# Unread matmuls and 128-partition operands at the start of an RWKV attention and wave-mixing kernel

## The chip, the cores and the metric

The kernel runs on one core of one Trainium2 chip. The metric is device time in microseconds of one execution. A core has TensorE (PE, matmuls; its weight loads are listed as PEld), VectorE (DVE), ScalarE (ACT), GpSimd (POOL) and SyncE (SP, which here only issues DMAs). Each engine works through its own instruction list in order and waits on semaphores for the others. TensorE writes to PSUM, which this kernel splits into eight banks.

## The reference

Inputs: r, k, v of shape (4, 8, 768, 48) (batch, heads, sequence, head size), w and u of shape (8, 48), a 384x384 matrix w_theta, two 768x768 matrices w_tok_r and w_tok_i, a 384x384 matrix w_ch; all float32.

```python
for t in range(S):                                     # per batch and head
    cur = einsum('bhd,bhe->bhde', u * k[t], v[t])
    y[t] = einsum('bhd,bhde->bhe', r[t], state + cur)
    state = w[:, :, None] * state + einsum('bhd,bhe->bhde', k[t], v[t])
x = y as (4, 768, 384)
theta = x @ w_theta
zr, zi = x * cos(theta), x * sin(theta)
u = x + w_tok_r @ zr + w_tok_i @ zi                    # over the sequence
out = u + max(u @ w_ch, 0)
```

w lies between 0.85 and 0.95. The recurrence is computed in chunks: powers of w are exp(position x log w), r and k are scaled by them, and matmuls take the place of the loop.

## The kernel before

The sequence is cut into 6 chunks of 128 positions; two chunks are one pair, so 4 batches give 12 pairs (g = 0 to 11). For each pair the front part loads k, r and v (tile `ld`), multiplies k and r by tables of powers (`Kw`, `Rw`, line 669), transposes them through TensorE (line 558, function flip) into banks, copies these out to `KT` and `RT` (lines 567 and 569), forms the scores (line 708), multiplies them by a causal mask (`mAT`, line 715), sums the state (lines 754 and 768) and adds past and present (lines 828, 839, 847). For the first four pairs v comes in two positions per row and is put in place by matmuls against a 0/1 matrix `place` (line 633; copied out at 641 and 643). Then theta (line 862), cosine and sine (867, 870), z (873), the mixing over the sequence (893), the residual (900), the channel product (916) and the result (920).

At the start log w must be had on every partition. w is loaded as one row (line 358), its logarithm taken on one partition (`lw_f`, line 409), and the function spread (line 418) multiplies a row of ones (1x128) with that row, in two halves of 192 columns, so that every partition of the bank `lw` holds all 384 values. The tables (line 474) are exponentials of that bank. The function stand (line 451) later puts log w upright for the decay over 256 positions. `w_f` and `lw_f` are rows in memory that later belongs to the tile z of batch 1.

The order of work is not that of the code. Every task is put on a plan with its engine, an estimated length, what it reads and writes, and which PSUM banks it takes. The method order simulates the engines with these estimates and takes, whenever an engine is free, the ready task with the lowest number in a written-out list, RANK. It charges matmuls 1.9 times their length while the plan's time is under SLOW_UNTIL = 10400 ns. The tasks are then issued in that order, each engine's instructions in a fixed sequence. A flag `port` marks VectorE and GpSimd tasks that share a memory port; a dependence is added between them so that they do not meet.

Before the change nothing stands in TensorE's list but work whose result is read.

Of the kernel before, what the change touches and what calls it, by code (L numbers as in the profile page):

```python
# [16 lines left out]
F32 = mybir.dt.float32  # L17
F16 = mybir.dt.float16
BF16 = mybir.dt.bfloat16
# [3 lines left out]
PE, DVE, ACT, POOL, SP = "PE", "DVE", "ACT", "POOL", "SP"  # L23
LAT = {PE: 230.0, DVE: 150.0, ACT: 250.0, POOL: 170.0, SP: 0.0}
SWITCH = 95.0
LANDING = 2000.0
SLOW_UNTIL = 10400.0
TURN_LATE = 1300.0

# [7 lines left out]
class Plan:  # L37
# [50 lines left out]
    def order(self):  # L88
# [15 lines left out]
        def release(xs, at):  # L104
            for x in xs:
                x.ready = max(x.ready, at)
                x.nwait -= 1
                if x.nwait == 0:
                    waiting[x.eng].append(x)
                    heapq.heappush(times, x.ready if x.ready > now else now + 1e-3)  # L110

        while times or dma_next < math.inf:
# [7 lines left out]
            while dma_at < now:  # L120
# [10 lines left out]
                if dma_at + need <= now + 1e-6:  # L131
                    dma_at += need
                    t = queues[q].pop(0)
                    todo[q] = queues[q][0].xfer if queues[q] else 0.0
                    t.end = dma_at + LANDING + (t.share[1] if q == 0 else 0.0)
                    release(t.users, t.end)
                else:
                    dma_at = now
            for e in engines:
# [14 lines left out]
                if e == PE:  # L154
                    ns += SWITCH if t.mode != last_mode else 0.0
                    ns *= 1.9 if now < SLOW_UNTIL else 1.0
                    last_mode = t.mode
# [97 lines left out]
def kernel(  # L255
# [13 lines left out]
    nc = tc.nc  # L269
    B, H, S, D = r.shape  # L270
    HD = H * D
    C = 128
# [7 lines left out]
    sb = ctx.enter_context(tc.tile_pool(name="sb", bufs=1))  # L280
    ps = ctx.enter_context(tc.tile_pool(name="ps", bufs=1, space=bass.MemoryType.PSUM))
    P = Plan(8)
    bank_t = [ps.tile([C, 512], F32, name=f"bank{i}") for i in range(8)]

    def bank(tok):
        return bank_t[P.bank_of[tok]]
# [4 lines left out]
    def ring(n, shape, dt, nm):  # L291
        return [sb.tile(shape, dt, name=f"{nm}{i}") for i in range(n)]
# [4 lines left out]
    pi2 = sb.tile([C, 1], F32, name="pi2")  # L297
# [1 line left out]
    wu = sb.tile([2 * HP, 2, Dp], F32, name="wu")  # L299
    tok_i = sb.tile([C, 1], mybir.dt.int32, name="tok_i")  # L300
    tok_f = sb.tile([C, 6], F32, name="tok_f")
    ones = sb.tile([1, C], F32, name="ones")
    gate = sb.tile([1, 1], F32, name="gate")
    place = sb.tile([C, 2, 2, C], BF16, name="place")
    rpow = sb.tile([C, 2, H, D], F32, name="rpow")
# [26 lines left out]
    zs = ring(2, [C, NCH, 2, HD], BF16, "z")  # L332
# [6 lines left out]
    WrT = sb.tile([C, NCH, S], BF16, name="WrT")  # L339
    WiT = sb.tile([C, NCH, S], BF16, name="WiT")  # L340

    w_f, lw_f = [zs[1].rearrange("p o t n -> p (o t n)")[:1, 2 * i * HD:2 * (i + 1) * HD]
                 .bitcast(F32) for i in range(2)]
    fins = [fin_all[:, i] for i in range(3)]
# [12 lines left out]
    def setup():  # L357
        P.add(SP, 420, lambda: nc.sync.dma_start(out=w_f, in_=w.rearrange("(o h) d -> o (h d)", o=1)),
              wr=["w_f"], prio=-1e7, xfer=-900)
# [6 lines left out]
        def fills():  # L366
            nc.vector.memset(pi2, math.pi / 2.0)
            nc.vector.memset(ones, 1.0)
        P.add(DVE, 120, fills, wr=["pi2", "ones"], prio=-101)
        P.add(ACT, 1400, lambda: nc.scalar.activation(warm, pi2, Act.Ln), wr=["warm"], prio=-99)  # L370

        def tok():
# [18 lines left out]
        def pads(ts):  # L391
            for t in ts:
# [3 lines left out]
              wr=["ident"], prio=-98)  # L396
        P.add(DVE, 200 * len(Rws), lambda: pads(Rws), wr=[("Rw", i) for i in range(len(Rws))],
              prio=-97)
        P.add(DVE, 200 * len(Kws), lambda: pads(Kws), wr=[("Kw", i) for i in range(len(Kws))],
              prio=-96)  # L400

        def mask():
# [1 line left out]
            nc.gpsimd.affine_select(  # L404
                out=mask01, in_=mask01, compare_op=Alu.is_ge, fill=0.0,
                base=-1, channel_multiplier=-1, pattern=[[1, C]])
        P.add(POOL, 600, mask, wr=["mask"], prio=-95)

        P.add(ACT, 550, lambda: nc.scalar.activation(lw_f, w_f, Act.Ln), rd=["w_f"],
              wr=["lw_f"], prio=-98)  # L410

        P.add(ACT, 1400, lambda: nc.scalar.activation(warm, pi2, Act.Exp), rd=["pi2", "lw_f"],
              wr=["warm"], prio=-97)

        for s in range(2):
            def spread(s=s):
                half = slice(s * HD // 2, (s + 1) * HD // 2)
                nc.tensor.matmul(bank("lw")[:, half], ones, lw_f[:, half],
                                 start=(s == 0), stop=(s == 1), skip_group_check=True)
            P.add(PE, 800, spread, rd=["lw_f", "ones"], acq=["lw"] if s == 0 else [],  # L420
                  use=[] if s == 0 else ["lw"], wr=[("lw", s)], prio=-98 + s, name="spread")
# [25 lines left out]
    def late_tables(rd):  # L447
        def stand():
            for h in range(H):
                q = h % 2 * Dp  # L450
                nc.tensor.matmul(bank("lwT")[q:q + D, h // 2:h // 2 + 1],
                                 lw_f[:, h * D:(h + 1) * D], ones[:, :1], start=(h < 2),
                                 stop=(h >= H - 2), skip_group_check=True)
        P.add(PE, 500, stand, rd=["lw_f", "ones"] + rd, acq=["lwT"], prio=3, mode=3,
              name="stand")

        def far():
            for hi in range(2):
                q = slice(hi * Dp, hi * Dp + D)
                nc.scalar.activation(w256[q], bank("lwT")[q, :HP], Act.Exp, scale=float(2 * C))  # L460
        P.add(ACT, 360, far, use=["lwT"], wr=["w256"], prio=3)

        def uw_fill():
            for hi in range(2):
                q = slice(hi * Dp, (hi + 1) * Dp)
                nc.vector.tensor_mul(uw[q, :, hi], wup[q, HP:], wup[q, :HP])
        P.add(DVE, 330, uw_fill, rd=["wup"] + rd, wr=["uw"], prio=3, port=True)
        table("kpow", kpow, 2, 5, rd)

    def table(key, dst, col, prio, rd=(), hs=range(H), s=None):  # L470
        h0, h1 = hs.start, hs.stop
        halves = [s] if s is not None else [0, 1]
        for c in range(2):
            P.add(ACT, act_ns((h1 - h0) * D, False) + 100, lambda c=c: nc.scalar.activation(
                dst[:, c, h0:h1].rearrange("p h d -> p (h d)"), bank("lw")[:, h0 * D:h1 * D],
                Act.Exp, scale=tok_f[:, col + c:col + c + 1]),
                rd=["tok_f"] + [("lw", i) for i in halves] + list(rd), use=["lw"],
                wr=[(key, c, i) for i in halves], prio=prio + 0.1 * c)
# [399 lines left out]
    def mixing(b, base):  # L878
        x, z = xs[b % 3], zs[b % 2]
        xi, zj = b % 3, b % 2  # L880
        for pr in range(NP):
# [42 lines left out]
            for ts_ in parts:  # L924
# [5 lines left out]
                    wr=[("out", b, pr, ts_.start)], prio=-2e6, xfer=520 * n)  # L930

    setup()
    front(0, 0)
    for b in range(B):
# [7 lines left out]
    for t, at in zip(P.tasks, RANK):  # L942
        t.prio = at
    order = P.order()
    made, before = nc.cur_bb.bb.instructions, None
    for t in order:
        n = len(made)
        t.fn()
        if not t.port:
            continue  # L950
        if t.eng == DVE:
            before = made[-1]
        elif before is not None:
            tc.add_manual_dep(made[n], before.name, mybir.DependencyInfo(
                mybir.DependencyClass.Sync, mybir.DependencyReason.DATA), reason="port")
            before = None
# [30 lines left out]
```

## Time and profile before

| What | us |
|---|---|
| three runs | 137.7, 138.62, 138.0 (median 138.0) |
| profiled execution | 138.1 |
| its span, first to last instruction | 136.4 |
| TensorE busy | 125.7 (92%) |
| VectorE busy | 111.1 (81%) |
| ScalarE busy | 73.1 (54%) |
| GpSimd busy | 62.0 (45%) |
| chain that ended last: TensorE, VectorE, DMA | 58%, 12%, 10% |
| read and written in memory off the core | 20.06 MB, 4.72 MB |

Times in the profile count from the first instruction of the span. A matmul's length includes its way through the array, so successive ones overlap; how fast TensorE works is read from the distance between starts, or by comparing matmuls of one shape. "[1.04 <-PE bank L708]" behind a line means that the engine was idle for 1.04 us before it and that the wait ended with TensorE's line 708. The spread's four passes (two halves, float32) start at 2.77 and end at 4.42. The next matmuls are four transposes at 5.83, one of 8 columns at 6.37, and four transposes at 7.47.

### The profile page before, as it was taken

How to read it: one execution, taken by the hardware profiler on the slowest of the kernel's cores; microseconds unless marked ns; L12 is line 12 of the kernel's file. 1: busy time of each engine (PE TensorE's matmuls, PEld its weight loads, DVE VectorE, ACT ScalarE, POOL GpSimd, SP SyncE). 2: the span in 40 equal slices, each digit the busy share in tenths (PEclk: the TensorE clock that was granted, in tenths of full speed). 3: DMA queues.
4: the chain of work that ended last, by engine and by line, in shares of the span. 5: the costliest groups of instructions: out<-in, count | busy, mean ns of one | idle time of the engine just before them, and what ended most of it. 6: DMA issues, size and time to landing. Idle time of an engine off the chain costs nothing.

```text
span 136.4 us, 4100 instructions
## 1 busy us (share of the span) xinstructions
PE 125.7 (92%) x1677; PEld 85.8 (63%) x1677; DVE 111.1 (81%) x209; ACT 73.1 (54%) x137; POOL 62.0 (45%) x54
## 2 busy tenths in 40 slices
PE   1589998999999999999999999999999999999970
PEld 1267876697577677757566666765666666666640
DVE  5199699998988799998999999999955799453390
ACT  7996599999756580687533308556450192500010
POOL 6027979984180658959379937690000000000000
PEclk9999999999999999999999999999999999999996
DMA  2999999999999999999999999989992842526245
GB/s 56 244 325 324 311 191 194 196 200 198 208 189 227 186 176 201 195 187 192 171 126 218 165 214 231 219 215 227 177 289 44 100 117 95 137 82 173 58 153 193
DMA packets 72637, 25.24 MB, mean 185 GB/s; under 512 B 67241, under 2 KB 72618, under 8 KB 72618
## 3 DMA queue, kind: packets, MB, share of 16 engines
q1 hardware_dynamic: 70186, 22.03, 82.5%
q0 software_dynamic: 2432, 2.95, 12.6%
q8 instruction: 13, 0.21, 0.7%
q14 instruction: 6, 0.05, 0.1%
HBM read 20.06 MB, written 4.72 MB: 182 GB/s over the span
## 4 chain that ended last, share of the span: by engine, by line
PE 58%; DVE 12%; DMA 10%; POOL 6%; SPq 6%; issue 5%; ACT 1%; POOLq 0%; ACTq 0%; DVEq 0%
PE bank L893 25%; PE bank L558 11%; PE bank L862 6%; PE bank L916 6%; DMA ld<-in_v_dram 4%; DVE mAT L715 4%; SPq L502 4%; DMA uu_all<-uu_all 3%; POOL Kw L669 3%; DMA ld<-in_r_dram 3%; PE bank L708 2%; PE bank L633 2%; PE bank L839 2%; POOL yd L739 2%; PE bank L768 2%
## 5 line engine op out<-in xcount | busy, mean ns | idle before, releaser
L893 PE MATMUL bank<-z,WrT 128*128 128x384 bf16 x144 | 46.9, 327 | 0.0
L893 PE MATMUL bank<-z,WiT 128*128 128x384 bf16 x144 | 46.8, 326 | 0.0
L715 DVE TENSOR_TENSOR mAT<-bank,mask 128x512 bf16<-128x512 f32 x48 | 30.7, 680 | 2.2 <-PE bank L708 2.1
L669 POOL TENSOR_TENSOR Kw<-ld,kpow 128x768 bf16<-128x768 f32 x9 | 16.3, 1812 | 13.7 <-DVE KT L567 6.1
L900 DVE TENSOR_TENSOR uu_all<-bank,x 128x384 bf16<-128x384 f32 x24 | 13.2, 552 | 8.8 <-PE bank L893 8.3
L893 PEld LDWEIGHTS <-WrT 128*128 128x128 bf16 x144 | 14.0, 97 | 8.0
L893 PEld LDWEIGHTS <-WiT 128*128 128x128 bf16 x144 | 14.1, 98 | 7.8
L669 POOL TENSOR_TENSOR Rw<-ld,rpow 128x768 bf16<-128x768 f32 x9 | 16.3, 1816 | 5.7 <-PE bank L708 2.4
L739 POOL TENSOR_TENSOR yd<-dg,vb 128x768 bf16<-128x768 f32 x10 | 14.7, 1472 | 6.5 <-DVE z L873 3.3
L870 ACT ACTIVATE trig<-bank 128x384 f16<-128x384 f32 x24 | 11.7, 498 | 10.2 <-PE bank L862 10.2
L920 DVE SCALAR_TENSOR_TENSOR fin_all<-bank,uu_all 128x384 f32<-128x384 f32 x24 | 12.6, 550 | 3.4 <-PE bank L916 3.4
L916 PE MATMUL bank<-Wch,uu_all 128*128 128x384 bf16 x72 | 14.7, 327 | 0.1
L867 ACT ACTIVATE trig<-bank,pi 128x384 f16<-128x384 f32 x24 | 13.7, 587 | 1.7 <-PE bank L862 1.7
L862 PE MATMUL bank<-Wth,xT 128*128 128x384 bf16 x72 | 14.4, 327 | 0.0
L873 DVE TENSOR_TENSOR z<-x,trig 128x1536 bf16<-128x1536 bf16 x12 | 13.0, 1084 | 0.4 <-ACT trig L867 0.4
L847 DVE TENSOR_TENSOR x<-bank,yd 128x384 bf16<-128x384 f32 x24 | 12.3, 547 | 0.7 <-POOL yd L739 0.5
L569 ACT ACTIVATE KT<-bank 128x1024 bf16<-128x1024 bf16 (+1 forms) x10 | 9.8, 982 | 5.1 <-PE bank L558 2.5
L569 ACT ACTIVATE RT<-bank 128x1024 bf16<-128x1024 bf16 (+1 forms) x9 | 8.7, 971 | 5.2 <-PE bank L558 5.2
L558 PE MATMUL bank<-ident,Kw 128*128 128x128 bf16 x96 | 8.9, 243 | 1.6 <-DVE Kw L669 1.4
L708 PE MATMUL bank<-RT,KT 64*128 64x128 bf16 x192 | 9.3, 226 | 0.0
L916 PEld LDWEIGHTS <-uu_all 128*128 128x128 bf16 x72 | 6.6, 98 | 4.2 <-DMA uu_all<-uu_all 0.5
L558 PE MATMUL bank<-ident,Rw 128*128 128x128 bf16 x96 | 8.4, 235 | 0.8 <-DVE Rw L669 0.8
(103 smaller groups left out, 186.9 us busy)
## 6 DMA issues: line engine op xcount, KB each, us to landing
ld<-in_r_dram SPq DMA_DIRECT2D x12, 384.0 KB, 5.4
out_dram<-fin_all SPq DMA_DIRECT2D x11, 384.0 KB, 2.7
ld<-in_k_dram SPq DMA_DIRECT2D x16, 192.0 KB, 5.1
ld<-in_v_dram SPq DMA_DIRECT2D x16, 192.0 KB, 4.9
ld<-in_k_dram SPq DMA_DIRECT2D x4, 384.0 KB, 4.8
ld<-in_v_dram SPq DMA_DIRECT2D x4, 384.0 KB, 5.6
fin_all<-in_moe_w_tok_r_dram POOLq DMA_DIRECT2D x1, 384.0 KB, 7.8
x<-in_moe_w_tok_i_dram POOLq DMA_DIRECT2D x1, 384.0 KB, 9.3
```

The lines of the kernel that those rows point to most:

```text
L558: nc.tensor.matmul(bank16(tok)[:, i * C:(i + 1) * C], s, ident, is_transpose=True, start=(i == 0), stop=(i == n - 1))
L569: nc.scalar.activation(dst, src, Act.Copy)
L669: eng.tensor_mul(X[:, :, hs, :D], src[:, :, hs], pw[:, :, hs])
L715: P.add(DVE, dve_ns(HP * C), lambda hi=hi, tk=tk, mAT=mAT: nc.vector.tensor_mul(mAT[:, hi], bank(tk[hi]).rearrange("p (h t) -> p h t", h=H ...
L739: eng.tensor_mul(yd.rearrange("p a h d -> p (a h) d"), wide(dg, D), vb.rearrange("p a h d -> p (a h) d"))
L862: nc.tensor.matmul(bank(th)[:, :HD], xT[:, t, dk, :], Wth[:, dk, :], start=(dk == 0), stop=(dk == ND - 1))
L867: P.add(ACT, act_ns(HD, False) + 65 + (1300 if g == 0 and t == 0 else 0), lambda th=th, t=t, trig=trig: nc.scalar.activation(trig[:, t, 0] ...
L873: P.add(DVE, dve_ns(4 * HD, 2.0) + 80, lambda trig=trig, pr=pr: nc.vector.tensor_mul(z[:, 2 * pr:2 * pr + 2], bc(x[:, 2 * pr:2 * pr + 2], ...
L893: nc.tensor.matmul(bank(tm)[:, :HD], (WrT, WiT)[ri][:, so, to * C:(to + 1) * C], z[:, so, ri], start=(part == 0 and i == 0), stop=(part == ...
L900: P.add(DVE, dve_ns(HD), lambda tm=tm, t=t, to=to, un=un: nc.vector.tensor_add(un[:, t], bank(tm)[:, :HD], x[:, to]), use=[tm], rd=[("x", ...
L916: nc.tensor.matmul(bank(tf)[:, :HD], uT[:, t, dk, :], Wch[:, dk, :], start=(dk == 0), stop=(dk == ND - 1))
L920: nc.vector.scalar_tensor_tensor(fin[:, t], bank(tf)[:, :HD], 0.0, un[:, t], op0=Alu.max, op1=Alu.add),
```

## The change

`ones` becomes 128x128. `lw_all` names all 128 partitions of the memory whose first partition is `lw_f`; VectorE sets it to zero before the logarithm is written there, and the spread multiplies the 128x128 ones with it: 127 of the 128 rows are zero, and the sums are the same. A tile `stuff` (128x256, bfloat16) is filled by GpSimd with 1.0 and, in every second column, -0.5. The function fill issues n matmuls of 256 columns with `stuff` as both operands into a bank that the plan holds to be free at that time; nothing reads the result. Six stand behind the second spread, ahead of the next TensorE task. replay goes once more through the order found by the plan, now charging 1.9 times only while the time is under FREE_FROM = 7400 ns, and notes for each TensorE task from when to when TensorE would wait for it. Ahead of each later task that begins before FILL_UNTIL = 17500 ns in that replay, fill is issued with as many matmuls as fit into the wait at 214 ns each (110 ns from 7400 ns on); these are 15 in all. The order of the tasks is the same as before.

```diff
+FILL_FIRST = 6
+FILL_UNTIL = 17500.0
+FREE_FROM = 7400.0
...
-    ones = sb.tile([1, C], F32, name="ones")
+    ones = sb.tile([C, C], F32, name="ones")
+    stuff = sb.tile([C, 2 * C], BF16, name="stuff")
...
+    lw_all = zs[1].rearrange("p o t n -> p (o t n)")[:, 2 * HD:4 * HD].bitcast(F32)
...
             nc.vector.memset(ones, 1.0)
-        P.add(DVE, 120, fills, wr=["pi2", "ones"], prio=-101)
+            nc.vector.memset(lw_all, 0.0)
+        P.add(DVE, 520, fills, wr=["pi2", "ones", "lw_f"], prio=-101)
...
-        P.add(POOL, 600, mask, wr=["mask"], prio=-95)
+            nc.gpsimd.memset(stuff, 1.0)
+            nc.gpsimd.memset(stuff.rearrange("p (a b) -> p a b", b=2)[:, :, 1], -0.5)
+        P.add(POOL, 1000, mask, wr=["mask"], prio=-95)
...
-                nc.tensor.matmul(bank("lw")[:, half], ones, lw_f[:, half],
+                nc.tensor.matmul(bank("lw")[:, half], ones, lw_all[:, half],
...
-                                 lw_f[:, h * D:(h + 1) * D], ones[:, :1], start=(h < 2),
+                                 lw_f[:, h * D:(h + 1) * D], ones[:1, :1], start=(h < 2),
...
+    held = {}
+    for t in order:
+        for b in t.uses:
+            a, e = held.get(b, (t.start, 0.0))
+            held[b] = (a, max(e, t.end))
+
+    def fill(since, until, n):
+        free = {}
+        for i in range(P.nbanks):
+            spans = [held[b] for b in held if P.bank_of[b] == i]
+            if all(e <= since or a >= until for a, e in spans):
+                free[i] = max([e for a, e in spans if e <= since], default=0.0)
+        if n < 1 or not free:
+            return
+        spare = bank_t[min(free, key=free.get)]
+        for _ in range(n):
+            nc.tensor.matmul(spare[:, :2 * C], stuff[:, :C], stuff, start=True, stop=True)
+
+    def replay():
+        free, done, left, gap, last_mode = dict.fromkeys((PE, DVE, ACT, POOL, SP), 0.0), {}, {}, {}, 0
+        port = 0.0
+        for t in order:
+            at = max([free[t.eng]] + [done[d] for d in t.deps])
+            for b in t.acq:
+                at = max(at, left.get(P.bank_of[b], 0.0))
+            if t.port:
+                at = max(at, port)
+            ns = t.ns
+            if t.eng == PE:
+                gap[t] = (free[PE], at)
+                ns += SWITCH if t.mode != last_mode else 0.0
+                ns *= 1.9 if at < FREE_FROM else 1.0
+                last_mode = t.mode
+            free[t.eng] = at + ns
...
+            done[t] = max(t.end, at) if t.xfer > 0 else at + ns + LAT[t.eng] - min(t.xfer, 0.0)
...
+        return gap
+
+    gap = replay()
+    idle_from, spreads = 0.0, 0
     made, before = nc.cur_bb.bb.instructions, None
     for t in order:
+        if t.eng == PE:
+            if spreads == 2:
+                fill(4e3, t.start, FILL_FIRST)
+            elif spreads > 2 and gap[t][1] < FILL_UNTIL:
+                since, until = gap[t]
+                fill(idle_from, t.start, int((until - since) / (214.0 if until < FREE_FROM else 110.0)))
+            spreads += t.name == "spread" or spreads >= 2
+            idle_from = t.start
         n = len(made)
         t.fn()
```

More of the change, by code (lines that the diff above doesn't have):

```diff
@@ L944 @@
     order = P.order()
+    held = {}
[30 more added lines that the diff above has]
+            free[t.eng] = at + ns
+            if t.port:
+                port = at + ns
+            done[t] = max(t.end, at) if t.xfer > 0 else at + ns + LAT[t.eng] - min(t.xfer, 0.0)
+            for b in t.uses:
+                left[P.bank_of[b]] = max(left.get(P.bank_of[b], 0.0), done[t])
+        return gap
+    gap = replay()
+    idle_from, spreads = 0.0, 0
     made, before = nc.cur_bb.bb.instructions, None
     for t in order:
+        if t.eng == PE:
[6 more added lines that the diff above has]
+            idle_from = t.start
         n = len(made)
```

## The prediction

> **What bounds the kernel now.** I read the page's busy shares and clock row first, then stretches of the span, then TensorE's and VectorE's instructions in order of time, then the chain and the waits. The page:
>
> ```profile
> PE 125.7 (92%) x1677; PEld 85.8 (63%) x1677; DVE 111.1 (81%) x209; ACT 73.1 (54%) x137; POOL 62.0 (45%) x54
> PEclk9999999999999999999999999999999999999996
> ```
>
> TensorE (PE) is busy nearly always, and the clock row shows a full clock from the start. The durations contradict that row. TensorE in order of time (start, length, line, shape; "xN" merges N matmuls):
>
> ```profile
> 10.67 1.46 PE L633 MATMUL bank<-v,place 128*128 128x384 bf16 x4
> ...
> 12.78 0.40 PE L731 MATMUL bank<-uw,PD 128*128 128x2 bf16 x8
> 13.10 0.81 PE L451 MATMUL bank<-ones,z 1*48 1x1 f32 x16
> 13.84 1.18 PE L768 MATMUL bank<-v,Kw 64*64 64x48 bf16 x32
> 14.95 1.03 PE L558 MATMUL bank<-ident,Rw 128*128 128x128 bf16 x8
> 15.91 0.61 PE L708 MATMUL bank<-RT,KT 64*128 64x128 bf16 x8
> ...
> 17.45 1.17 PE L633 MATMUL bank<-v,place 128*128 128x384 bf16 x4
> ...
> 18.86 0.48 PE L633 MATMUL bank<-v,place 128*128 128x384 bf16 x2
> ...
> 20.16 0.62 PE L558 MATMUL bank<-ident,Rw 128*128 128x128 bf16 x8
> ```
>
> Compare like with like. Eight transposes of 128 columns (L558) take 1.03 us at 14.95 and 0.62 us at 20.16. Single L633 matmuls of 384 columns last 525 ns at 17.45 and 17.77, then 368 at 18.09, then 327 at 18.29, and start 320 ns apart before and 160 ns apart after. So TensorE runs at half rate until about 18.2 us and at full rate from there. From 8.48 to 18.09 it has no gap over 0.15 us beyond its own work; the chain of work that ended last lies on matmuls from 7.47 to 19.36 almost without a break. That is 9.6 us at half rate, and up to 4.8 us if all of it ran at full rate. That is the prize. Who would be late next? VectorE (DVE):
>
> ```profile
> 13.65 1.13 DVE L669 TENSOR_TENSOR Kw<-ld,kpow 128x768 bf16<-128x768 f32 x1
> ...
> 15.15 0.36 DVE L805 TENSOR_TENSOR T<-bank,N 128x192 f32<-128x192 f32 x1
> 16.56 1.29 DVE L715 TENSOR_TENSOR mAT<-bank,mask 128x512 bf16<-128x512 f32 x2 [1.04 <-PE bank L708]
> ...
> 19.98 0.56 DVE L643 CAST vb<-bank 128x384 bf16<-128x384 f32 x1 [0.20 <-ACT dg L736]
> ```
>
> Between 8.6 and 20 us VectorE stands idle for TensorE only once worth naming, 1.04 us before the mAT products, and 0.20 us at 19.98. Stretches after that (busy us of PE, PEld, DVE, ACT, POOL):
>
> ```profile
> 20.00:24.00 4.00, 3.61 (x74) 2.65 (x67) 4.00 (x8) 3.72 (x8) 3.91 (x4) 1.00 1.18 192
> 24.00:28.00 4.00, 3.85 (x103) 2.88 (x101) 4.00 (x10) 3.96 (x7) 3.98 (x5) 1.00 1.15 197
> 28.00:49.00 21.00, 21.00 (x300) 15.21 (x297) 18.44 (x31) 15.77 (x28) 11.13 (x8) 1.00 1.13 196
> 49.00:96.00 47.00, 46.17 (x737) 31.66 (x736) 46.24 (x82) 24.35 (x46) 31.94 (x21) 1.00 1.23 198
> ```
>
> From 20 to 28 VectorE is full (8.00 of 8.00) and TensorE is the one that waits. From 28 to 49 TensorE is full, from 49 to 96 both nearly, and after 96 it is a run of matmuls. So time won on TensorE before 18 us passes through VectorE's full stretch: the end moves by what VectorE wins, not by what TensorE wins.
>
> **The change part by part.** All sums are against the profiled execution, 138.1 us (span 136.4, 1.7 around it); the median shown, 138.0, is 0.1 lower.
>
> *Setup fills.* VectorE's new fill of log w is 384 columns on 128 partitions. A 128-column fill (L393) lasts 0.17 and the next begins 0.14 later, so 0.42. Filling `ones` on 128 partitions instead of 1 is free by the rows (1x128, 8x128 and 128x128 all 0.17). VectorE's setup work ends at 2.95 and it is next needed at 5.21, so 0.42 is hidden with 1.8 us to spare. One point is open: SyncE's small w load at 1.71 must follow the fill of wu, which ends at 1.24 and would end at 1.66, just as SyncE's k issue ends (1.67): cost 0. But the chain view ties that load to a VectorE instruction that ends at 2.05; if that is right, every later load slips 0.42. I take 0 (the fill named in the code decides) and keep 0.42. GpSimd's two fills of `stuff`: 0.21 for 128 columns (L403), 0.53 for 512 (L424), so 0.32 plus 0.21 to 0.53 for the strided one. `place` then is ready at 3.8 instead of 3.2 and is first read at 10.67: hidden.
>
> *Spread with 128 rows.* The four passes of L418 (1 row, 192 columns) start 320 ns apart. Rows do not change a start-to-start time elsewhere (L558 with 128 rows: 106 ns per 128 columns at half rate; L708 with 64 rows in pairs: the same). I take no cost; double, 1.65, as the far end would push the first transposes from 5.83 to 6.1.
>
> *Six unread matmuls.* 256 columns are two thirds of an L633 matmul: 213 ns at half rate, 107 at full. Six from about 4.2 are 1.28, done by 5.5; the next matmul starts at 5.83 when VectorE's Kw lands. Cost 0.
>
> *Fifteen more.* 15 x 107 = 1.6 us at full rate, 3.2 us at half. They sit ahead of tasks that the kernel's own plan thinks will wait. At full rate TensorE has about 4.8 us less to do there, so they displace nothing but waiting: 0, at worst the 1.6 us.
>
> *Will the rate rise earlier?* The rows ask what came before 18.2. From 14.95 to 18.09 nearly all is full-height work (128 rows, 128 columns of weights). From 12.78 to 14.95 there was none: two-column, one-row and 64*64 matmuls. From 10.67 to 12.78 there was full-height work for only 2.1 us, and the rate stayed low. So about 3 us of full-height work seems to be needed; the change puts full-height work from 2.77 to 5.5 (2.7 us), then transposes and fills. My estimate is a rise between 6 and 10 us.
>
> [...]
>
> *What it is worth.* TensorE's late step is the score product at 15.91 (L708), for which VectorE waits until 16.56. At full rate it cannot come before GpSimd's Rw is done (12.15 + 1.81 = 13.96): transposes 14.02 to 14.45, scores to 14.8, so VectorE goes on at 15.5, when T ends: 1.04 won. This holds if the rate rises by 13, since only about 1 us must be won on matmuls before 14.95. At 19.98 the put matmuls come early too: 0.20 more. ScalarE's RT copy at 16.02 moves to 14.7, so it does not take over. VectorE is then 1.24 ahead through 28. Two things cap this. The v load read at 22.43 by ScalarE landed at 21.05, margin 1.4. And:
>
> ```profile
> 45.37 1.81 POOL L669 TENSOR_TENSOR Kw<-ld,kpow 128x768 bf16<-128x768 f32 x1 [4.23 <-DMA ld<-in_r_dram]
> ```
>
> GpSimd's Kw waits for a load; it ends at 47.18, and its transposes start at 47.79. If that load does not move, the win shrinks to 0.6. SyncE issues it at 40.70 in 0.57 us, without the 1.1 us of a full queue, so it partly moves with the rest: between 0.6 and 1.24, I take 1.0. **138.1 - 1.0 = 137.1 us.**
>
> **The rivals.**
> *B: TensorE alone sets the end.* It won 4.8 and pays 10 fills (those not in the idle from 6.4 to 7.5), 1.1: 3.7 won, 134.4 us. For it: 92% busy. Against it: VectorE's 8.00 of 8.00 from 20 to 28. Part of VectorE's length is waiting for GpSimd's port (two L466 of 64x4 take 1.56), so some of this may come: 134.4 to 136.6.
> *C: the win is eaten* by the w load's 0.42 and by the loads at 45: 0.6 - 0.42 = 0.2 won, 137.9 (137.6 to 138.4 with nothing won).
> *D, the other side: the rate does not rise before 13.* Then the fills run at 213 ns in a stretch without gaps. Five fit in 6.4 to 7.5, ten x 0.213 = 2.1 lie on the chain: 140.2; if the rate rises some 3 us earlier than now, half of that is won back: 138.9. The point that decides is whether the scores at 15.91 move below 15.9. For it: the rate stayed low through 9.6 us without gaps. Against: none of that was 3 us of full-height work.
>
> One way into D has a chance of its own, 0.08 of D's 0.23: transposes (L558) do nothing for the rate, so that after 5.5 us only the fills in the gaps do, and it rises no earlier than now: 140.2. The stretch before 18.2, over half transposes, is what keeps that chance small. [...]
>
> **How the numbers follow.** Forecast 0.46 (136.3 to 137.6), B 0.18, C 0.13, D 0.23. A measurement of this kernel can tell about 1%, 1.4 us. Faster by more: B, and the part of the forecast that wins over 1.4 (0.15), 0.33. Slower: most of D, 0.18. The rest, 0.49. The range goes from the middle of B, 135.4, to the middle of D, 139.6, and leaves about 0.2 out.
>
> **What would show it.** L633 matmuls at 10.67 of 323 to 327 ns and eight L558 in 0.62 from about 10 us on: the rate rose. VectorE's idle before mAT at 16.56 gone: the step that pays. First r load issued at 3.23 as now: no slip. Matmuls of 256 columns starting 107 ns apart, with TensorE waiting after them: the fills are free. I am wrong if scores at 15.91 do not move, or if the end moves by over 2 us, which would say VectorE's full stretch was not full.

## The result and the profile after

The changed kernel's median is 139.04 us (137.92 to 140.13, 19 runs), that of the kernel before 138.25 us on the same chip. The ratio is **1.0062, 95% interval 1.0035 to 1.0088**: a little slower, by about 0.8 us, where 1.0 us faster was forecast. It lies inside the range and inside the 1% either way, and beyond what these many runs leave to chance. The profiled execution took 139.07 us with a span of 137.4; before it was 138.1 and 136.4. So both profiled executions differ by 1.0 us, in the direction of the medians, and are laid side by side. Some executions of every kernel take over 1.5% longer than its fastest one; the ratios in this document leave them out, the medians do not, and the profiles of spread_only, nowth_closed and tail108 are of such executions.

The page after (busy shares, the instruction queue, the chain's shares by engine):

```profile
PE 125.3 (91%) x1698; PEld 84.9 (62%) x1698; DVE 112.3 (82%) x210; ACT 73.1 (53%) x137; POOL 62.5 (46%) x56
...
q8 instruction: 13, 0.21, 0.6%
...
PE 49%; DMA 17%; DVE 14%; POOL 9%; SPq 5%; issue 3%; ACT 1%; POOLq 0%; DVEq 0%
```

TensorE has 21 more matmuls and 21 more weight loads, 42 instructions. DMA's share of the chain is 17%, 10% before: the end hangs more on transfers than it did. TensorE after, in order of time (L566 is L558 before, L969 the fills):

```profile
5.83 0.61 PE L566 MATMUL bank<-ident,Kw 128*128 128x128 bf16 x4
...
6.58 0.43 PE L969 MATMUL bank<-stuff 128*128 128x256 bf16 x2
7.33 0.40 PE L566 MATMUL bank<-ident,Rw 128*128 128x128 bf16 x4 [0.33 <-DVE Rw L677]
...
8.03 0.82 PE L969 MATMUL bank<-stuff 128*128 128x256 bf16 x6
```

Four transposes take 0.61 us at 5.83 and 0.40 at 7.33. The fill at 6.58 lasts 319 ns, the next one 273. **The rate rises between 6.58 and 6.73**, where it rose at 18.2 before. VectorE after:

```profile
15.31 1.28 DVE L723 TENSOR_TENSOR mAT<-bank,mask 128x512 bf16<-128x512 f32 x2
...
18.80 0.56 DVE L651 CAST vb<-bank 128x384 bf16<-128x384 f32 x1 [0.28 <-PE bank L641]
```

The mAT products that began at 16.56 after 1.04 us of waiting begin at 15.31 without any. All that VectorE does from there to 28 us is 1.2 to 1.3 us earlier than before. So the forecast's step is there. Where does it go?

Compare the starts of the same TensorE instructions in the two traces' records (after minus before): -2.42 us at 18.09, -1.18 at 23.16, -1.01 at 27.28, **-0.36 at 30.68**, -0.07 at 68.71, +0.06 at 76.88, **+1.01 at 83.21**, +0.99 at 98.20 and so on to the end. There are two main places: one near 30 us where most of the win goes, and one between 77 and 83 us where a loss as large as the forecast's win comes. Between them 0.37 us more goes at 68.71, behind a product Rw of GpSimd that starts at 66.8 us in both traces (66.85 and 66.77).

**The first place.** GpSimd's queue casts the mixing's weights on their way in (w_theta's 147456 float32 values are 288 KB in the view, two bytes each). The view of DMA issues from 14 to 24 us, of the kernel before (target, engine that issues, KB each, median us from issue to landing):

```profile
fin_all<-in_moe_w_tok_r_dram POOLq DMA_DIRECT2D x1, 384.0 KB, 7.8
x<-in_moe_w_tok_i_dram POOLq DMA_DIRECT2D x1, 384.0 KB, 9.3
z<-in_moe_w_tok_r_dram POOLq DMA_DIRECT2D x1, 384.0 KB, 7.9
```

and of the kernel after:

```profile
fin_all<-in_moe_w_tok_r_dram POOLq DMA_DIRECT2D x1, 384.0 KB, 8.6
x<-in_moe_w_tok_i_dram POOLq DMA_DIRECT2D x1, 384.0 KB, 10.1
z<-in_moe_w_tok_r_dram POOLq DMA_DIRECT2D x1, 384.0 KB, 9.4
```

They are issued 0.1 to 0.8 us earlier and take 0.8 to 1.5 us longer: the z cast landed at 29.58 before and lands at 30.27 after. The DMA engines have little room in this stretch. Their share is 1.15 and 1.13 before and 1.16 and 1.06 after (24 to 28, 28 to 49 us), and in both traces these casts land 2.2 to 2.3 us apart, 384 KB each, some 170 GB/s.

How much of the 0.7 us comes from the change? In the records of both kernels the semaphore of each of the eight casts is raised sixteen times, that of the z cast from 28.23 to 29.58 before and from 27.70 to 30.27 after; a raise is read here as a part that has landed. After, the matmuls that waited for it start at 30.32, behind the last raise. Of the z cast, fifteen parts had landed by 29.41 before and by 29.43 after, the sixteenth by 29.58 and by 30.27. So one lagging part makes the difference, and the kernel before has it too in a second profile (before_again, below: 29.58 and 30.96). What does hold in every profile is that the landing does not follow the issue. In the 18 profiles of this document that have all casts, this one is issued between 20.8 and 22.6 us and lands between 29.4 and 31.7; the five that are issued by 21.1 us land at 29.7 to 30.9. After's chain of work that ended last (start, length, what) goes through that landing:

```profile
20.86 9.41 DMA z<-in_moe_w_tok_r_dram
...
30.32 0.51 PE bank L566 x6
```

Before, the chain at 29 us is on TensorE (L558, 2.13 us from 29.05). After, TensorE is early and the weights are late.

**The second place.** The waits of the stretch from 78 to 86 us, before and then after (engine and line, what it waited for, us in total, times, longest):

```profile
POOL Rw L669 <- PE bank L708: 2.4, 1, 2.4
```

```profile
POOL Rw L677 <- DMA ld<-in_r_dram: 3.4, 1, 3.4
```

GpSimd's Rw waits for another thing than before: the r load issued at 75.16 landed at 80.55; after it is issued at 75.79 and lands at 82.19. Rw starts at 82.34 instead of 81.27, its transposes at 84.22 instead of 83.21, and the 1.0 us stays to the end. The issues and landings of the loads slip from about 53 us on. Stretches of after (busy us of PE, PEld, DVE, ACT, POOL; granted clock, DMA share, GB/s):

```profile
52.00:53.00 1.00, 1.00 (x20) 0.69 (x20) 1.00 (x3) 0.00 (x0) 0.48 (x1) 1.00 2.15 186
53.00:54.00 1.00, 1.00 (x14) 0.66 (x12) 1.00 (x3) 0.00 (x0) 1.00 (x1) 1.00 1.57 47
54.00:55.00 1.00, 1.00 (x17) 0.74 (x15) 1.00 (x3) 0.18 (x1) 1.00 (x2) 1.00 0.26 51
```

The rate of transfer falls to 47 and 51 GB/s; before it is 174 and 191 in these two microseconds. In the records, 20 packets of a transposing DMA (uu_all, issued at 50.2) last up to 1.97 us each at 52.9, just where a packet of the instruction queue begins (53.1). The page's instruction queue moves 0.21 MB in 13 packets, 16 KB each; for 3396 TensorE instructions that is about 63 bytes each, or some 260 instructions in a packet, an estimate that counts the whole queue as TensorE's (pad128, below, adds 256 TensorE instructions and one packet). These packets last 0.9 to 1.5 us. Before, the corresponding one came at 53.72, and no packet near it lasted long. The transposing DMA lands at 55.86 instead of 54.44, the v load before it at 55.02 instead of 53.65, and the transfers issued behind it up to 65 us land 0.3 to 2.4 us late where the record has their landing.

Two things speak against this stall as the cause of the 1.0 us. The kernel before has such stalls as well, and deeper ones: its rate falls to 43, 11 and 30 GB/s in the microseconds from 64, 71 and 89. The one from 71, before:

```profile
71.00:72.00 1.00, 1.00 (x26) 0.83 (x26) 1.00 (x3) 0.00 (x0) 1.00 (x2) 1.00 0.19 11
```

And of the r load that Rw waits for, fifteen of the sixteen parts had landed by 80.96, early enough for the old start at 81.27; only the last came at 82.19. Before, all sixteen landed between 80.37 and 80.55. So most of this loss is again one lagging part. A fetch ran beside it from 79.73 to 80.82, but one ran from 79.66 to 80.80 before, where nothing lagged; why a part lags stays open.

### The profile page after: what moved, and what is told of

Read it like the earlier page. It is cut to its first block, busy times and chain, and to the rows that moved or that the text cites. A ratio compares the mean times of both kernels' runs of the same rounds, so it can differ in the third digit from the quotient of the medians.

```text
span 137.4 us, 4145 instructions
## 1 busy us (share of the span) xinstructions
PE 125.3 (91%) x1698; PEld 84.9 (62%) x1698; DVE 112.3 (82%) x210; ACT 73.1 (53%) x137; POOL 62.5 (46%) x56
## 4 chain that ended last, share of the span: by engine, by line
PE 49%; DMA 17%; DVE 14%; POOL 9%; SPq 5%; issue 3%; ACT 1%; POOLq 0%; DVEq 0%
PE bank L901 24%; DMA z<-in_moe_w_tok_r_dram 7%; PE bank L566 6%; PE bank L870 6%; DMA ld<-in_v_dram 6%; PE bank L924 5%; SPq L503 4%; DVE mAT L723 4%; DMA ld<-in_r_dram 4%; POOL Rw L677 3%; DVE fin_all L928 2%; POOL yd L747 2%; PE bank L716 2%; PE bank L847 2%; PE bank L762 2%
## 5 line engine op out<-in xcount | busy, mean ns | idle before, releaser
L723 DVE TENSOR_TENSOR mAT<-bank,mask 128x512 bf16<-128x512 f32 x48 | 30.7, 680 | 1.4 <-PE bank L716 1.3
L677 POOL TENSOR_TENSOR Kw<-ld,kpow 128x768 bf16<-128x768 f32 x9 | 16.3, 1816 | 12.7 <-DVE PD L730 6.4
L924 PE MATMUL bank<-Wch,uu_all 128*128 128x384 bf16 x72 | 14.6, 326 | 0.0
L881 DVE TENSOR_TENSOR z<-x,trig 128x1536 bf16<-128x1536 bf16 x12 | 12.8, 1063 | 0.4 <-ACT trig L875 0.4
L566 PE MATMUL bank<-ident,Rw 128*128 128x128 bf16 x96 | 7.6, 220 | 1.6 <-DVE fin_all L928 0.8
L716 PE MATMUL bank<-RT,KT 64*128 64x128 bf16 x192 | 8.8, 218 | 0.0
L870 PEld LDWEIGHTS <-xT 128*128 128x128 bf16 x72 | 6.3, 97 | 4.0 <-issue 0.4
```

The source lines that it names most:

```text
L566: nc.tensor.matmul(bank16(tok)[:, i * C:(i + 1) * C], s, ident, is_transpose=True, start=(i == 0), stop=(i == n - 1))
L677: eng.tensor_mul(X[:, :, hs, :D], src[:, :, hs], pw[:, :, hs])
L723: P.add(DVE, dve_ns(HP * C), lambda hi=hi, tk=tk, mAT=mAT: nc.vector.tensor_mul(mAT[:, hi], bank(tk[hi]).rearrange("p (h t) -> p h t", h=H ...
L870: nc.tensor.matmul(bank(th)[:, :HD], xT[:, t, dk, :], Wth[:, dk, :], start=(dk == 0), stop=(dk == ND - 1))
L881: P.add(DVE, dve_ns(4 * HD, 2.0) + 80, lambda trig=trig, pr=pr: nc.vector.tensor_mul(z[:, 2 * pr:2 * pr + 2], bc(x[:, 2 * pr:2 * pr + 2], ...
L924: nc.tensor.matmul(bank(tf)[:, :HD], uT[:, t, dk, :], Wch[:, dk, :], start=(dk == 0), stop=(dk == ND - 1))
```

## The experiments

After this reading three theories stood against each other.

- **F**: the 42 added TensorE instructions cost, whatever they do; they change when the 16 KB fetches come and what these meet.
- **R**: the early full rate itself costs, since early work makes transfers collide.
- **C**: the early rate's win dies at the landings of the token-weight casts; take a cast away and it lives.

All ratios are against the kernel before on the same chip, with a 95% interval; "rate up" is the time in us at which matmuls of one shape begin to take the shorter length in that kernel's profile.

### Instructions without an early rate: pad21

```diff
+NPAD = 21
...
+            nc.tensor.matmul(spare[:, :2], ident[:1, :], ident[:1, :2], start=True, stop=True)
...
+        if t.eng == PE:
+            if spreads == 2:
+                pad(4e3, t.start, NPAD)
```

Nothing else of the change is in it: 21 one-row, two-column matmuls behind the second spread, in idle time, 42 instructions.

> The kernel before, with 21 unread matmuls of one row and two columns behind the spread, where TensorE waits anyway (4.2 to 5.8 us): 42 more TensorE instructions, weight loads counted, the same number as the change adds, and no full-height work. The rate should rise at 15 to 18 us as before. Theory F (fetches): TensorE's instruction fetches, 13 transfers of 16 KB that each hold one DMA engine for about 1 us, are moved by the added instructions and then meet other loads; expects the change's whole loss, 1.006 of before. Theory R (rate): the early rate itself re-times loads and transposes to the worse; expects 1.000.

Measured: 138.93 us, **1.0027 (0.9996 to 1.0058)**, rate up at 18.2. TensorE stands as before to within 0.2 us until 76 us, then +0.46 at 76.9 and +1.00 at 83.21, the change's own loss. Its chain:

```profile
82.34 1.82 POOL Rw L670
84.16 0.05 issue
84.21 0.62 PE bank L559 x8
```

The same Rw starts at the same 82.34 as in the changed kernel, and the stall of the transposing DMA is there at 52.7 us. The r load's first fifteen parts land by 81.43 and the last at 82.18. So in this profile the second loss needs no early rate. The ratio by itself stays open, since its interval reaches below 1.

### The rate's parts alone: three512, six, spread_only

three512 keeps the 128-row spread and puts three fills of 512 columns in place of the six, none in the gaps (6 instructions); six leaves out the 15 in the gaps (12); spread_only leaves out all fills (0).

```diff
-            elif spreads > 2 and gap[t][1] < FILL_UNTIL:
-                since, until = gap[t]
-                fill(idle_from, t.start, int((until - since) / (214.0 if until < FREE_FROM else 110.0)))
```

> The change with three unread matmuls of 512 columns behind the spread in place of six of 256 (the same 1.28 us at half rate) and none in the gaps: 6 more TensorE instructions instead of 42. The rate should rise at 6 to 10 us as with the change. Theory F expects 0.995 to 1.000 of before (the loss gone, 0 to 0.7 us of the early win left). Theory R expects 1.006, as the change.

> The change without the 15 unread matmuls in the gaps: 12 more TensorE instructions. The rate should rise at 6 to 10 us and, if the 15 are needed to hold it, fall again before 18. Theory F expects between three512 and the change, 0.997 to 1.004. Theory R expects 1.006 if the rate holds.

> The change with the 128-partition spread and its fills alone, no unread matmul: no more TensorE instructions than before. 1.3 us of full-height work should not raise the rate, so it rises at 15 to 18 us. Both theories expect 1.000; a rise before 10 us would say that the spread alone does it.

Measured: three512 138.24 us, 1.0007 (0.9977 to 1.0038), rate up at 12.1. six 138.28 us, 0.996 (0.9928 to 0.9993), rate up only at 17.6. spread_only 138.78 us, 1.000 (0.9967 to 1.0033), rate up at 20.4. The spread costs nothing that shows. In three512's profile TensorE is 1.2 us ahead at 27 us and 1.25 behind at 83.21: the same r load has fifteen parts landed by 81.49 and the last at 82.42. So the second loss comes with 6 added instructions too, in a kernel whose time is that of the kernel before; it cannot be put down to the 42. six looked like a version that beats the kernel before, so it ran once more:

> Six once more: is it faster than the kernel before? 0.996 if so; 1.000, as pad7 with nearly the same number of instructions, if its first measurement was at the edge by chance.

138.32 us, 1.0023 (0.9991 to 1.0055): the first was at the edge of chance, and no gain is shown. Six fills alone do not raise the rate before 17 us in either profile (17.6, 18.2); a rise before 12 us was seen only with fills in the gaps.

### Same number of instructions, rate early or late: pad7 and open14, pad40 and after_pad19

open14 raises the rate with seven fills of 512 columns (three behind the spread, one and three later); pad7 has as many instructions (14) but one-row ones. after_pad19 is the changed kernel with 19 one-row matmuls more, pad40 the kernel before with 40 (80 added in both).

```diff
+            if spreads == 4:
+                fill(idle_from, t.start, 1)
+            if spreads == 6:
+                fill(idle_from, t.start, 3)
```

> The kernel before with 7 unread one-row matmuls behind the spread, 14 more TensorE instructions, and no full-height work: the rate should rise at 15 to 18 us. Six (12 more instructions, and in its profile no early rate either) came at 0.996. Theory F: 0.996, and in the profile the fetch near 53 us does not fall into the transposing DMA issued near 50. Theory R: 1.000.

> The change with 7 unread matmuls of 512 columns (3 behind the spread, 1 and 3 in the first two gaps) in place of 21 of 256, the same length at half rate: 14 more TensorE instructions, rate up at 6 to 10 us. Theory F: as pad7, 0.996, since the early win is lost at the token weights' landing near 30 us anyway. Theory R: 1.006, as the change.

> As pad7 with 40 unread one-row matmuls, 80 more TensorE instructions, rate up late. Theory F: another place of the fetches and so another time, not told beforehand in size, within 0.994 to 1.008, and the same as after_pad19. Theory R: 1.000.

> The change with 19 unread one-row matmuls more in the gap near 6.8 us, 80 more TensorE instructions than before, rate up early. Theory F: the same ratio as pad40 within 0.004, since only the number of instructions counts. Theory R: 1.006, as the change.

| kernel | added | rate up | us | ratio (95%) |
|---|---|---|---|---|
| pad7 | 14 | 12.8 | 138.53 | 0.9998 (0.9963 to 1.0034) |
| open14 | 14 | 7.0 | 139.03 | 1.0014 (0.9975 to 1.0053) |
| pad40 | 80 | 18.4 | 139.5 | 1.0052 (1.0011 to 1.0094) |
| after_pad19 | 80 | 6.5 | 139.66 | 1.0073 (1.0037 to 1.011) |

The number of added instructions orders them, not the rate. pad40, with a late rate, is as slow as the change. The early rate brings no gain that shows in either pair. Unplanned, pad7's rate rose at 12.8 us; it was 2.1 us ahead at 18.09 us and level by 39.7. So a rise without fills loses its win too.

### Without one cast: nowth_open and nowth_closed

The cast of w_theta is left out and its tile set to 0.02, in the changed kernel (open) and in pad21 (closed). Theta's weights are then a constant, so the output is not the reference's; 288 KB of transfer are gone from the full stretch.

```diff
+            nc.gpsimd.memset(Wth, 0.02)
...
-        cast(dst, src.rearrange("(o p) n -> p o n", p=C), [key], prio,
+        cast(None if key == "Wth" else dst, src.rearrange("(o p) n -> p o n", p=C), [key], prio,
```

> The change without the cast of w_theta (288 KB, the first transfer of the token weights' queue); the tile is set to a constant by GpSimd in its idle time at the start, so theta is not the reference's. Theory C (the early win dies because TensorE has caught up with the token weights, whose transfers fill the DMA engines from 18 to 39 us): their landings come about 1.8 us earlier, TensorE's wait for the transfer into z near 30 us goes, TensorE is still about 1 us ahead of nowth_closed at 31 to 35 us, and the ratio of the two kernels is 0.991 to 0.997. If the win goes for another reason, the two are the same within 0.003 or this one is the slower.

> pad21 (42 more TensorE instructions, no full-height matmul, rate up late) without the cast of w_theta, in the same way. The partner of nowth_open with the same number of instructions. Theory C: slower than nowth_open by 0.4 to 1.2 us; otherwise the same.

Measured: open 137.74 us, 0.9957 (0.9917 to 0.9997); closed 137.89 us, 0.9933 (0.9895 to 0.9971). C wanted open clearly ahead of closed, and it is not. In open's profile the win lives past the first place (-1.26 us at 17.8, -1.01 from 23 to 68 against the kernel before), as C has it, shrinks to -0.65 at 68.7 and -0.44 at 86.2, and is gone at 93.7, behind another stalled transposing DMA (92.05 us, packets of up to 1.7 us). So the landings are where most of the win was lost in the change's profile, and without that cast it is lost at later places. As an account of the total, C falls.

This profile also shows the price of the forecast's rival D. The rate rose only at 11.1 us here, and the fills before it ran at half rate:

```profile
8.20 1.48 PE L970 MATMUL bank<-stuff 128*128 128x256 bf16 x6
9.48 0.63 PE L567 MATMUL bank<-ident,Rw 128*128 128x128 bf16 x4
```

The transposes at 8.48 stand at 9.48: 1.0 us late, by six fills. With the rate up from 11.1 this is made good by 14.6.

### How the cost grows: pad128 and pad108

256 and 216 added instructions, all in idle time before 7.4 us, on their own one-row operand; the rest is the kernel before.

```diff
+            if spreads == 0:
+                pad(0.0, 4e3, 48)
+            elif spreads in (2, 4):
+                pad(4e3, t.start, 42 if spreads == 2 else NPAD)
```

(pad108 has 40, 38 and 30 for 48, 42 and 38.)

> The kernel before with 128 unread one-row matmuls in TensorE's idle time before 7.4 us: 256 more instructions, just one 16 KB fetch, so all later fetches come at the same tasks as before, with one more early. Theory F as a matter of place: 1.000 to 1.003, below pad40 (1.0052). If it is the number of added instructions as such that costs: 1.008 or more.

> 108 unread one-row matmuls in TensorE's idle time before 7.4 us, 216 more instructions: every later fetch comes some 40 instructions later than in the kernel before, so the one near 53.7 falls behind the transposing DMA that lands at 54.4. If the place of the fetch decides: 1.000 to 1.004, clearly below pad128 (1.0108). If the number of instructions does: 1.007 to 1.011.

pad128: 139.87 us, **1.0108 (1.0066 to 1.015)**, with one fetch more, at 7.43 us. Its page:

```profile
q8 instruction: 14, 0.23, 0.7%
```

pad108: 139.76 us, 1.0088 (1.005 to 1.0126). It was to tell whether it is the place of the fetch near 50 us that costs (1.000 to 1.004) or the number (1.007 to 1.011). The ratio is the one that the number calls for, and the fetch near 50 us falls as the cause.

Number and place are still not told apart, for these kernels move another fetch. Their first one comes at 7.43 (pad128) and 8.8 us (pad108 and its second profile) instead of 14.55, in the middle of the first burst of loads. In these three profiles the r load issued near 5.5 us lands at 11.70 to 11.92, before at 10.40, and the loads behind it up to 18.9 us stay 1.0 to 1.6 us late. The burst's rate (last number) falls, before and then in pad108_again:

```profile
11.00:12.00 1.00, 1.00 (x5) 0.48 (x4) 0.95 (x4) 0.38 (x1) 0.16 (x1) 1.00 1.17 325
11.00:12.00 1.00, 1.00 (x4) 0.25 (x2) 0.53 (x1) 0.00 (x0) 0.98 (x1) 1.00 0.87 198
```

So one fetch in this burst is a second possible price of 216 and 256 instructions, and no run parts it from their number. pad40's price is open in the same way: its first fetch comes at 11.88, and the load that landed at 12.79 before lands at 14.33, after loads that were 0.4 us late already.

### Once more: before_again, pad21_again, after_again

> The kernel before, unchanged, as a control: ratio 1.000, and a second profile of it. Theory F expects the first transposing DMA (issued near 50 us) to land near 54.4 again, with no fetch in it, and a span near 136.4.

> pad21 once more (42 more TensorE instructions, no full-height matmul), beside the change on one chip. Theory F: 1.003 to 1.006, the transposing DMA lands at 55.4 or later, span near 137.4. If only the rate counted: 1.000.

> The change once more, beside pad21 on one chip. Its ratio less that of pad21_again is what the rate and the length of the fills cost beyond the instructions: 0.000 to 0.002 by theory F, 0.006 if the rate does it all. A profile in which its rate rises late would show the fills at half rate on the chain, about 1 us late at 9.5 us.

The kernel before, run once more as a kernel of its own, gives 138.72 us, 1.0006 (0.9969 to 1.0044). pad21 again: 139.51 us, **1.0078 (1.0043 to 1.0113)**. The change again: 139.84 us, 1.0104 (1.0064 to 1.0144), rate up at 6.96. So 42 instructions without an early rate cost 0.3% and 0.8% in two series; the interval of the first reaches below 1, that of the second does not. What was to tie it to one event did not hold: before_again's first transposing DMA landed at 56.97 without a stall there, later than in the changed kernel, in a kernel that is no slower; and pad21_again's profile has no stall at 52 us and a span of 136.1 although its median is slow. after_again's profile has the stall near 53 us, but there the r load of the second place lands whole by 80.83, Rw starts at 81.12, and nothing is lost at 83 us. One profile cannot stand for the median here.

### Behind all work: tail108 and pad108_again

The same 108 matmuls, but at the end of TensorE's list, against the kernel with them at the start:

```diff
+    pad(max(t.end for t in order), 1e9, NPAD)
```

> The 216 added TensorE instructions of the pad108 kernel (108 unread one-row, two-column matmuls), but at the very end of TensorE's list, behind the last channel product (132.1 us of 136.4 in the trace of before), where TensorE has nothing else to do; everything ahead of them is the kernel before. Theory 'mere number' (a longer TensorE list costs wherever the instructions stand): 1.006 to 1.011, as pad108. Theory 'ahead of the work' (instructions cost only because all later ones, and with them the fetches of 16 KB, stand elsewhere against the loads and the transposing DMAs): 0.997 to 1.003, since the fetches fall as in the kernel before up to 121.9 us and the load chain ends by 96. One caveat for both: if the added matmuls do not end before the last output lands, some 3 us of them at most lie beside the last output DMA; at 30 ns each they end by 135.3.

> The same 108 matmuls at the start, on the same chip as the kernel with them at the end. Both theories: 1.005 to 1.012, as the first time (1.0088). Should it come out below 1.003, the cost of added instructions differs from chip to chip, and the kernel with them at the end tells nothing.

pad108_again: 139.76 us, 1.0078 (1.0035 to 1.0121), as the first time. tail108: 138.76 us, **1.0028 (0.9999 to 1.0056)**; in its profile they run from 133.79 to 136.64 and end 1.8 us before the span does:

```profile
133.79 2.85 PE L962 MATMUL bank<-tiny 1*128 1x2 bf16 x108
```

By the ratios they cost at the end about a third of what they cost at the start. "Mere number" in full (1.006 and up) falls. "Ahead of the work" is favoured, at the upper end of its 0.997 to 1.003; the two intervals still overlap, so a small price of the number itself is left open. The first loads fit it: tail108's first fetch is at 14.69, and the r load that landed at 10.40 before lands at 10.42.

## Why the prediction was wrong, by its steps

- **TensorE at half rate to 18.2 us although the clock row says full**: right, and shown by what a rise at 6.6 does to the same matmuls. The kernels without fills in the gaps show that the time of the rise varies from one profile to the next (12.1 to 20.6 us), so 18.2 was one draw of many; the prediction took it as fixed.
- **Setup fills, place and spread at no cost**: right. The r load is issued at 3.23 us as before, the w load does not slip, spread_only is 1.000.
- **Fills**: 213 ns apart at half rate and 109 at full, priced at 213 and 107. In the profile after only the transposes at 8.48 are late behind them, by 0.2 us that is made good by 9.0; when the rate came late (nowth_open), six of them cost 1.0 us, a little under D's 213 ns each.
- **The rise between 6 and 10**: right in the changed kernel (6.6; again 6.96), 11.1 in nowth_open. Its reason, about 3 us of full-height work, is not borne out. The stretch from 14.95 to 18.09 that it was read from holds 0.7 us of 64-row matmuls (15.91 and 16.32), so 2.4 us of full-height work, little more than the 2.1 that had not sufficed. And six has the same full-height work as the change up to 6.58 us and rises at 17.6 and 18.2. What sets the time stays open. D's own way, in which transposes do nothing for the rate (0.08), is parted from the others by no run; by it the rise was to come no earlier than in the kernel before (18.2), and it came at 6.6, 6.96 and 11.1 us.
- **Worth 1.24 us through VectorE up to 28 us**: right, 1.25 at mAT and 1.2 to 1.3 through 27. B, TensorE alone, is out: TensorE had won 2.4 us at 18 us, 1.0 of it was left at 27 and none at the end. B's wait for GpSimd's port: of the two L466 products one took 161 ns and the other 1390, ending at 11.18 beside GpSimd's Kw (9.35 to 11.16); after they took 162 and 1335, the long one ending at 11.06 beside Kw (9.21 to 11.03). (The middle of B's 134.4 to 136.6 is 135.5, not 135.4; nothing hangs on it.)
- **What caps it: this step failed.** I named the v load at 21.05 and the load at 45.37, and kept 1.0 of 1.24. The v load moved with the rest (19.97). The load at 45.34 did not move at all; its issue took 0.57 us before and 0.65 after, against 1.09 to 1.25 for the issues from 4.34 to 12.94 before and 0.35 to 0.81 for those ahead of them, and that a full queue makes the difference was an estimate. But the win was mostly gone by then: the token-weight casts, which the prediction did not look at, landed 0.3 to 0.7 us later although issued earlier, and left 0.36 at 30.7 us, about 0.1 at 69. The 0.7 is one lagging part, and so partly the luck of this profile; that the landing does not come earlier with the issue holds in all 18 profiles. The DMA share over 1.1 and the 196 GB/s in the very stretches I quoted were reason to ask whether an earlier issue would land earlier. Rival C (the win is eaten) describes this profile at 69 us, though not by its own terms: the 0.42 of the w load was never paid.
- **What 42 more TensorE instructions cost: a term that was missing.** I priced the 21 matmuls by their time on the array and found cover for it, and priced their fetching at nothing without saying so. Without any early rate, 42 cost 0.27 and 0.78%, 80 cost 0.52%, 216 cost 0.88 and 0.78%, 256 cost 1.08%; 0 to 14 cost nothing that shows (0.996 to 1.0023). By the ratios that is some 0.4 to 1.1 us for 42, where the change lost 0.8. Rival D was to be the way to slower; the loss came without it.

How the 42 instructions cost is not shown. In the profiles of the change and of pad21 a fetch meets a transposing DMA, the loads slip, and Rw waits; but the kernel before has such stalls too, Rw waits for one lagging part of a load, three512 has that without any cost, and before_again, pad21_again and after_again do not fit one fixed place. For 216 and 256 there is a visible place: a fetch in the first burst of loads, which then land 1.0 to 1.6 us late in all three profiles. That it makes up their medians is argued. The runs favour that the instructions cost more ahead of the work than behind it. In the trace of the kernel before, the thirteen fetches leave TensorE itself without a visible wait: it has one gap over 0.3 us after 8 us (0.39 at 23.16, for VectorE's PD). But the runs above put 0.3 to 1.1% on 42 to 256 instructions added ahead of the work, in a kernel whose DMA share is 1.13 to 1.23 from 20 to 96 us.

Does the early rate cost something too? At equal numbers of instructions, early against late: 1.0014 to 0.9998, 1.0104 to 1.0078, 1.0073 to 1.0052, 0.9957 to 0.9933 on the same chip each, and 1.0062 to 1.0027 on two. Early is 0.16 to 0.35% behind in all five by these ratios, within the intervals of each; by the medians of all executions the nowth pair stands the other way round. No pair shows a win; a small loss (R) stays open.

## What to carry to other kernels

Time won early in a kernel must be followed to the next thing that does not move with it. Here that was a stretch with a DMA share of 1.06 to 1.16: four casts issued 0.1 to 0.8 us earlier landed in it 0.7 us later. In such a stretch, price an earlier issue at an unchanged landing. Filler matmuls are instructions too; in a kernel like this one (3354 TensorE instructions, DMA share over 1) count them, and give few wide ones rather than many narrow ones (seven of 512 columns, 14 instructions, came with a rise at 7.0 us and no price that shows). And where one profile is laid beside another, ask how far two profiles of one kernel differ before a stall in one of them is made the cause. A late transfer is worth a look at its sixteen landings: one lagging part tells another story than a load that is late as a whole.

## What the runs showed of the hardware

- The clock row of the page shows full speed from the first slice although matmuls run at half rate up to the rise; only lengths or distances of one shape tell (384 columns: 525 ns long and 320 apart, against 327 and 163). A matmul outlasts the distance to the next start by 205 to 208 ns at half rate and 163 to 164 at full, alike for 128, 256 and 384 columns (L558, the fills, L633; before and after).
- The time of the rise is not the kernel's own: 12.1 to 20.6 us in the fifteen profiles without fills in the gaps (three512 and pad108_again at the ends), 6.5 to 7.0 in four with them, 11.1 in a fifth. One and the same kernel rose between 12.7 and 14.8 (pad108) and at 20.6 (pad108_again). Once the rate fell again: in nowth_closed, TensorE waited 2.9 us up to 26.66 and ran at half rate from about 28.0 to 31.4.
- A fetch of 16 KB lasts 0.9 to 1.5 us in the profiles before and after. Some 20 of a transposing DMA's 256-byte packets lasted 0.9 to 2.0 us at a time (before: at 63.6, 70.6, 88.5 and 108.9 us; after: 52.9 and 88.7), and the core's transfer rate beside three of them fell to 43, 11 and 30 GB/s for a microsecond (before, from 64, 71 and 89). A fetch ran beside all of these but the one at 63.6.
- The work that waited for a load or a cast went on after the last of its sixteen parts (matmuls at 30.32 after 30.27, Rw at 82.34 after 82.19, in the profile after), and one part lagged the other fifteen by 0.8 to 1.4 us (30.27 after 29.43, 82.19 after 80.96 there; 30.96 after 29.58 in before_again).
- A fetch in the burst of loads at the start was followed by loads 1.0 to 1.6 us late and a rate of 187 to 215 GB/s instead of 325 from 11 to 12 us (pad108, pad108_again, pad128).
